# First batch, weight conversion and sixteen feed-forward steps laid out as one list of ranked tasks

## The chip, the cores and the metric

The kernel runs on one core of a Trainium2 chip. A core has a matrix engine (TensorE, "PE" in the profile, its weight loads "PEld"), a vector engine (VectorE, "DVE"), a scalar engine (ScalarE, "ACT"), a general engine (GpSimd, "POOL") and a queue that issues transfers (SyncE, "SP"). Each runs its own instructions in order and waits for the others through semaphores. The metric is the device time of one execution in microseconds (us); a change is judged by the median over several executions.

## The reference

```python
def _attn_ref(q, k, v):                      # q, k, v: 8 batches, 8 heads, 576 tokens, 64
    q_d = q.reshape(B, H, Sd, factor, D).mean(axis=3)      # factor 4: 144 coarse tokens
    ...                                      # k_d, v_d in the same way
    out_d = sm_attn(q_d, k_d, v_d)           # softmax attention over the coarse tokens
    out_up = np.repeat(out_d, factor, axis=2)
    mask = np.abs(pos[:, None] - pos[None, :]) < factor    # each token sees 7 neighbours
    scores = scale * np.matmul(q, k.transpose(0, 1, 3, 2))
    scores = np.where(mask, scores, -1000000000.0)
    ...                                      # softmax
    return out_up + np.matmul(attn, v)

def _moe_ref(x, w_in, w_out, alpha):         # x: 4608 tokens, 512; 2048 hidden
    h = x @ w_in
    g = np.maximum(h, 0.0) + alpha * np.minimum(h, 0.0)
    return g @ w_out
```

The attention of all heads, laid side by side, is the x of the feed-forward. The two weight matrices arrive as 64-bit floats, everything else as 32-bit floats.

## The kernel before

**Feed-forward.** The 4608 tokens are cut into 18 chunks of 256 and the hidden layer into 8 pieces of 256. A step s is one piece of one chunk (s = 8 x chunk + piece): `hidden` (24 matmuls, L752), then `slopes` on ACT, `larger` on DVE (L764), `split` into a high part on ACT and a low part on POOL, then `product` (12 matmuls of 512 columns, L796). Below h(s) and o(s) stand for the hidden and the product of step s. Each operand is held as a high and a low part, so each of the two products is three matmuls. There are 144 steps. A chunk's o sums eight steps in two banks of PSUM.

**Weights.** A 64-bit weight is rebuilt as a 32-bit one by integer operations in `make` (L161): an absolute value on ACT (L184), a clamp and a shift on DVE (L188, L189), sign and low bits on DVE (L193, L194), the high part on ACT (L199, L203) and the low part on DVE (L207, L211). Each of the 16 pieces (8 of w_in, 8 of w_out) holds 1024 elements a partition. Pieces 0 to 4 of each matrix are made whole with their intermediate in SBUF; pieces 5 to 7 in halves, with the intermediate in PSUM banks q and l (L180). Loads (L145, L149) go through three slots.

**First batch.** Batch 0 fills chunks 0 and 1 and 64 tokens ("rest") of chunk 2. It runs over four pairs of heads (`first_batch`, L363). For a pair the queries and keys are turned on PE (L425) and copied by ACT; the neighbour attention runs on PE in nine windows of 64 tokens (L445, L493, L509); the coarse sums of q and k are made on DVE (L453, L455) and turned again on PE (L460); the coarse result is weighed on PE (L501), copied, and added to the neighbour result on DVE (L512).

**Later batches.** The coarse attention is `down` (L224), four times a batch: six loads, two additions each on POOL (L241, L242), a turn on PE (L250), scores, exponentials, weighing (L297). The neighbour attention is `local` (L566), by units of 192 tokens, three units a batch, nearly all on DVE: products with keys (L591), sums (L595), products with values (L643, L647), running sums (L650, L653). Its result is turned on PE (L659), joined with the coarse result on DVE (L671) and placed as a chunk's operand by ACT (L685) and POOL (L69). Units count from 3, the first of batch 1; chunk 2 is the rest of batch 0 and unit 3. `FAR` says how many of a unit's seven neighbours are summed on POOL.

**Order.** Two ways of setting the order stand side by side. The first batch, the first ten pieces and the first `down` are emitted one after another and ordered by the scheduler of the language. From there on each function is given a time counted in steps by `at`, the list is sorted by it, and each engine runs its part in that order: h(s) at s - 1.95, o(s) at s + 0.6, the units at the times of `UNITS`, the last six pieces from `T0_DEC` on. The steps go in order of s, chunk 0 first, then chunk 1.

## Time and profile before

| | us |
|---|---|
| median of 3 runs | 1029.55 |
| lowest, highest | 1028.1, 1031.91 |
| the profiled execution | 1026.39 |
| its span in the trace | 1024.5 |

The span lies inside the execution: 1.89 us stand outside it. In the profile's rows the first number is the start or the busy time, and "[x <-Y]" is the idle time of the engine before the row and what ended it. In the tables by stretch, each engine's busy time stands with its number of instructions, then the granted clock of PE as a share of full speed, then the share of the DMA engines and GB/s.

### The profile page before, as it was taken

Reading aid. Unit: us, or ns where it says so; the run is one execution under the profiler, and the core shown is the slowest. Engines: PE = TensorE matmul, PEld = TensorE weight load, DVE = VectorE, ACT = ScalarE, POOL = GpSimd, SP = SyncE. Lnnn points to the kernel's source line nnn. Section 1 sums busy time; section 2 is a strip of 40 time slices with the busy share of each in tenths; the row PEclk is TensorE's granted clock in tenths of the full one; section 3 lists DMA queues with packets and bytes.
Section 4 is the critical chain, followed back from the end, with each engine's and each line's share of the span. In section 5 each row is a group of like instructions: output and inputs, shape, how many; then the busy total and the mean of one; then the engine's idle time right before and its main releaser. Section 6 shows DMA issues by size and latency. Waiting matters only on the chain.

```text
span 1024.5 us, 17852 instructions
## 1 busy us (share of the span) xinstructions
PE 960.5 (94%) x6402; PEld 853.0 (83%) x6402; DVE 831.8 (81%) x1346; ACT 560.4 (55%) x1484; POOL 487.7 (48%) x612
## 2 busy tenths in 40 slices
...
GB/s 184 228 141 246 111 126 110 96 109 85 115 100 95 106 75 86 109 93 102 107 84 74 92 107 77 116 90 80 104 98 81 93 78 62 73 36 21 1 21 20
DMA packets 59549, 98.25 MB, mean 96 GB/s; under 512 B 19910, under 2 KB 25286, under 8 KB 59462
## 3 DMA queue, kind: packets, MB, share of 16 engines
...
## 4 chain that ended last, share of the span: by engine, by line
PE 74%; DVE 12%; DMA 4%; ACT 3%; issue 2%; SPq 2%; POOL 2%; ACTq 0%; DVEq 0%; POOLq 0%
PE h L752 34%; PE o L796 33%; PE s L263 2%; PE pv L297 2%; DVE temp L193 2%; DMA raw<-in_moe_w_in 1%; PE xp L659 1%; DMA ld<-in_v 1%; PE pT L287 1%; DVE temp L194 1%; DMA k<-in_k 1%; DVE t L764 1%; DVE qk L591 1%; SPq L393 1%; DVE temp L188 1%
## 5 line engine op out<-in xcount | busy, mean ns | idle before, releaser
L69 POOL TENSOR_TENSOR gl<-t,gh 128x512 fp32r<-128x512 f32 x144 | 186.4, 1295 | 312.9 <-ACT gh L769 281.5
L760 ACT ACTIVATE t<-h,slope 128x256 f32<-128x256 f32 x288 | 136.3, 473 | 205.4 <-PE h L752 163.6
L72 POOL TENSOR_TENSOR ld<-ld 72x256 f32<-72x256 f32 x168 | 130.8, 779 | 158.4 <-DMA ld<-in_q 88.6
L752 PE MATMUL h<-xh,wih 128*128 128x256 f32 x1152 | 191.9, 288 | 0.7 <-ACT xh L518 0.7
L764 DVE TENSOR_TENSOR t<-h,t 128x512 f32<-128x512 f32 x144 | 99.0, 687 | 114.8 <-ACT h L761 112.9
L796 PE MATMUL o<-woh,gh 128*128 128x512 f32 x576 | 187.5, 407 | 0.4 <-ACT woh L203 0.4
L752 PE MATMUL h<-xl,wih 128*128 128x256 f32 x1152 | 184.3, 282 | 1.4 <-POOL xl L69 1.4
L752 PE MATMUL h<-xh,wil 128*128 128x256 f32 x1152 | 185.0, 283 | 0.0
L796 PE MATMUL o<-woh,gl 128*128 128x512 f32 x576 | 181.1, 396 | 0.9 <-POOL gl L69 0.9
L796 PE MATMUL o<-wol,gh 128*128 128x512 f32 x576 | 181.4, 396 | 0.2 <-DVE wol L211 0.2
L752 PEld LDWEIGHTS h<-xh,wih 128*128 128x128 f32 x1152 | 164.2, 191 | 10.7 <-issue 1.8
L752 PEld LDWEIGHTS h<-xl,wih 128*128 128x128 f32 x1152 | 157.5, 190 | 1.6 <-POOL xl L69 1.6
L752 PEld LDWEIGHTS h<-xh,wil 128*128 128x128 f32 x1152 | 158.4, 191 | 0.0
L769 ACT CAST gh<-t 128x512 fp32r<-128x512 f32 x144 | 89.1, 619 | 120.7 <-DVE t L764 71.4
L595 DVE TENSOR_REDUCE ls<-qk 128x12 f32<-128x768 f32 (+1 forms) x126 | 136.4, 1082 | 2.8
L796 PEld LDWEIGHTS o<-woh,gl 128*128 128x128 f32 x576 | 108.2, 188 | 27.5 <-POOL gl L69 1.3
L796 PEld LDWEIGHTS o<-wol,gh 128*128 128x128 f32 x576 | 108.1, 188 | 26.8 <-DVE wol L211 1.1
L761 ACT ACTIVATE h<-h,sign 128x256 f32<-128x256 f32 x288 | 126.4, 439 | 0.0
L650 DVE TENSOR_TENSOR lb<-lb,pv 128x384 f32<-128x384 f32 x202 | 113.9, 564 | 5.5
L796 PEld LDWEIGHTS o<-woh,gh 128*128 128x128 f32 x576 | 98.1, 189 | 16.2 <-issue 2.2
L647 DVE TENSOR_TENSOR pv<-v,lb 128x1152 f32<-128x1152 f32 x84 | 93.6, 1115 | 2.6
L591 DVE TENSOR_TENSOR qk<-k,qp 128x768 f32<-128x768 f32 (+1 forms) x78 | 84.1, 1079 | 0.6 <-DMA k<-in_k 0.6
(146 smaller groups left out, 1108.6 us busy)
## 6 DMA issues: line engine op xcount, KB each, us to landing
...
```

The costliest lines, as they stand in the source:

```text
L69: nc.gpsimd.tensor_tensor(o, a, b, op=ALU.subtract)
L72: nc.gpsimd.tensor_tensor(o, a, b, op=ALU.add)
L591: nc.vector.tensor_tensor(st["pr"][:, :nd], window(tiles[u, "k"], half, d0, nd), st["qp", half].unsqueeze(1).to_broadcast([128, nd, 2, 192 ...
L595: nc.vector.tensor_reduce(out=st["s"][:, half, d0:d0 + nd, :].rearrange("p a b -> p (a b)"), in_=st["pr"][:, :nd].rearrange("p a h (t d) - ...
L647: nc.vector.tensor_tensor(st["pr"][:, :nd], window4(tiles[u, "v"], half, d0, nd), prob(half, d0, nd), op=ALU.mult)
L650: nc.vector.tensor_tensor(st["acc"], st["acc"], st["pr"][:, i], op=ALU.add)
L752: nc.tensor.matmul(ph[:, j], w[:, m, 128 * o:128 * o + 128], x[:, m, :], start=(i == 0), stop=(i == 11))
L760: nc.scalar.activation(t[:, j], hs[st][:, j], AF.Copy, scale=slope[:, f:f + 1])
L761: nc.scalar.activation(hs[st][:, j], hs[st][:, j], AF.Copy, scale=sign[:, f:f + 1])
L764: nc.vector.tensor_tensor(gs[st], hs.pop(st), gs[st], op=ALU.max)
L769: nc.scalar.copy(gh, t)
L796: nc.tensor.matmul(po, g[:, j, 128 * m:128 * m + 128], wo[w][n][:, o, :], start=(f == 0 and i == 0), stop=(f == NF - 1 and i == 2))
```

## The change

- Everything up to step 15 becomes one list of tasks, each with an engine, a duration, the tasks it depends on and a rank. `planned` lays them out: again and again it takes the task that can begin first, by rank where several can begin at once. The resulting begin times, divided by `STEP`, are merged with the timed events of the rest of the kernel, and each engine runs the merged order. The scheduler of the language no longer orders any of it. Pair tasks have ranks 0 to 3, the ACT tasks of the conversion 4, the steps 5 to 6.75, the coarse attention of batch 1 5.2 to 6.1, and the DVE tasks of the conversion 8 and up.
- The steps of chunks 0 and 1 are interleaved: chunk 1 follows two pieces behind chunk 0 (`LAG`). Chunk 0 sums in the banks q and l, chunk 1 in the banks o.
- Pieces 0 to 5 are made whole, 6 and 7 in halves; no intermediate is in PSUM any more.
- In the first batch the coarse sums of q and k are taken by DVE from the turned tiles in PSUM (`reduce`), the second turn goes, and the coarse result is summed in the same bank as the neighbour result by matmuls that repeat each coarse column four times (`values`), so the addition on DVE goes.
- In `down` of batch 1 the sums of q and k are taken by 32 small matmuls on PE (`gather`) in place of additions on POOL and four turns.
- Unit 3 works in SBUF (`in_sbuf`), since banks q and l hold chunk 0; one of its seven neighbours, not two, is summed on POOL; the load of unit 4's queries is issued later. The masks are built later (`UNITS[3] - 3.0`).
- The later units start 2.2 (unit 3) or 2.6 steps later on the list, and the steps from 16 on 2.6 (`DELAY`).

```diff
-PTB = 1
-FPT = ('ooo', 'ooo', 'ooo', 'oqo')
-FPV = ('ooo', 'ooo', 'ooo', 'qlq')
-EM = 'bbba'
-ORDER = 'i0 a0 a1 b0 o0 a2 b1 a3 b2 i1 b3 o1 i2'
-N_EARLY = 5
-FIRST = (-1.3, 0.3, 3.0, 5.7)
-T0_DEC, D_DEC = 0.5, 0.56
-UNITS = {3: 7.5, 4: 12.2, 5: 17.4, 6: 22.7, 7: 28.0}
+ORDER = 'a0 i0 a1 b0 a2 b1 i1 a3 b2 o0 b3 i2 o1 i3 o2 i4 o3 i5 o4 o5 i6 i7 o6 o7'
+LAG = 2
+DOWN1 = (5.2, 0.3)
+STEP = 6.3
+DELAY = 2.6
+UNITS = {3: 9.7, 4: 14.8, 5: 20.0, 6: 25.3, 7: 30.6}
 U_STEP = 5.92
 BY_HALF = (5, 9, 13, 17, 21)
-FAR = {3: 2, 4: 2, 5: 2, 6: 2}
+FAR = {4: 2, 5: 2, 6: 2}
...
+            if which == 0 or n < 3:
+                t = weights_temp[0][:, slot % 2, 0:512 * len(cs)]
             else:
-                t = bank("ql"[turns[1] % 2], f"temp{which}{fp}{c}").bitcast(I32)
-            turns[1] += 1
+                t = late.tile([128, 512], I32, tag=("x", "xf", "vt")[slot % 3], name=f"temp{which}{fp}{c}")
...
+        def gather(i):
+            if i == 0:
+                if hp == 0:
+                    new_od(b)
+                st["pt"] = bank("d", f"qkT{nm}")
+            for g in range(2):
+                for f in range(FACTOR):
+                    for e, r in enumerate(halves):
+                        nc.tensor.matmul(st["pt"][r, (2 * i + g) * 72:(2 * i + g) * 72 + 72], st[2 * i + e][:, g, f, :],
+                                         ident[:72, :72], start=(f == 0), stop=(f == FACTOR - 1))
...
+            got = []
+            for i in range(6):
+                got.append(task("SP", 0.7, lambda i=i: load(i), *logs["ld"].get(6 * hp + i - LDB, []), *logs["got"][-1:], pr=place["d"]))
+                logs["got"].append(got[-1])
+                if i == 1 or i == 3:
+                    x = i // 2
+                    m = plan("PE", 1.3, lambda x=x: gather(x), *got[-2:], *(turn_of("d") if x == 0 else [m]))
+                    logs["ld"][6 * hp + i - 1] = logs["ld"][6 * hp + i] = [m]
+                elif i > 3:
+                    logs["ld"][6 * hp + i] = [plan("POOL", 1.3, lambda i=i: fold(i), got[-1], *free("v", S2B))]
+            vs = logs["ld"][6 * hp + 4] + logs["ld"][6 * hp + 5]
+            y = plan("ACT", 1.1, operands, m, *free("qd", 1))
+            rings["d"].append((m, [y]))
...
+            def reduce(x, b):
+                if ("s", x) not in g:
+                    g["s", x] = st.tile([128, 2, 72], F32, tag=f"fs{x}", name=f"fs{x}{hp}")
+                nc.vector.tensor_reduce(out=g["s", x][:, b], in_=g["ph", x, b][:, 0:288].rearrange("p (t a) -> p a t", t=4),
+                                        axis=AX.X, op=ALU.add)
...
+            def values(a, b):
+                ps = g["pv", a] = ps_o.tile([128, 512], F32, tag="po", name=f"fpv{hp}{a}")
+                n = 16 * (b - a)
+                for x in range(2):
                     for e, r in enumerate(halves):
...
+                        nc.tensor.matmul(ps[r, 0:4 * n].rearrange("p (n r) -> p n r", r=4), g["vd"][:, e, x],
+                                         g["th", x][:, SD * e + 16 * a:SD * e + 16 * b].unsqueeze(2).to_broadcast([72, n, 4]),
+                                         start=(x == 0), stop=False)
+                for w in range(a, b):
                     for e, r in enumerate(halves):
...
-                    xs.rearrange("p (a r) -> p a r", r=4),
-                    ps[:, 0:WIN * nw].rearrange("p (a r) -> p a r", r=4),
-                    odf[:, 16 * w0:16 * (w0 + nw)].unsqueeze(2).to_broadcast([128, 16 * nw, 4]), op=ALU.add)
...
+                        nc.tensor.matmul(ps[r, WIN * (w - a):WIN * (w - a) + WIN], vw[hp][:, w, e, :],
+                                         g["pT"][:, w, 64 * e:64 * e + 64], start=False, stop=(w == b - 1))
...
+            def upper(a):
+                if a == 8:
+                    nc.scalar.copy(rest[:, hp, :], g["pv", a][:, 0:WIN])
+                else:
+                    nc.scalar.copy(operand(a // 4)[0][:, hp, :], g["pv", a][:, 0:4 * WIN])
+
+            def lower(a):
+                hi, lo = (t[:, hp, :] for t in operand(a // 4))
+                nc.vector.tensor_tensor(lo, g["pv", a][:, 0:4 * WIN], f32(hi), op=ALU.subtract)
...
+        def in_sbuf():
+            lb = one.tile([128, 256], F32, tag="s2q", name=f"lb{u}")
+            st["pw"] = lb[:, 0:84].rearrange("p (a b c) -> p a b c", a=2, b=7)
+            st["mx"], st["sm"], st["rs"] = (lb[:, 84 + 12 * i:96 + 12 * i].rearrange("p (a c) -> p a c", a=2)
+                                            for i in range(3))
+            acc = late.tile([128, 2, 3, 64], F32, tag="pp", name=f"acc{u}", bufs=2)
+            st["acc"] = acc
+            for half in range(2):
+                st["qp", half] = tiles[u, "q"][:, :, 3 * half:3 * half + 3, :].rearrange("p h t d -> p h (t d)")
...
+            at(when["total", str((1, 5, 2))] + 0.04 if u == 3 else half_done + 0.03 if by_half else t0 + 1.0, load_q, u + 1)
...
+            outs[c] = [bank("ql"[m], f"o{c}_{m}") if c == 0 else ps_o.tile([128, DM], F32, tag="po", name=f"o{c}_{m}")
+                       for m in range(T // 128)]
...
+    def planned():
+        begin, end, free = [0.0] * len(tasks), {}, {}
+        left = list(range(len(tasks)))
+        while left:
+            best = {}
+            for i in left:
+                engine, us, f, deps, pr = tasks[i]
+                if all(d in end for d in deps):
+                    r = max([end[d] + (2.0 if tasks[d][0] == "SP" else 0.15 if tasks[d][0] != engine else 0.0)
+                             for d in deps] + [0.0])
+                    t = max(r, free.get(engine, 0.0))
+                    best[engine] = min(best.get(engine, (1e9,)), (t, pr, i))
+            t, _, i = min(best.values())
+            engine, us = tasks[i][:2]
+            begin[i], end[i] = t, t + us
+            free[engine] = t + us
+            left.remove(i)
+        return begin
...
+        if whole:
+            wait = slots[-3] if len(slots) >= 3 else []
+        else:
+            wait = list(last) + halves_of.get((fp, c), [])
+        got = task("SP", 4.0 * size, lambda slot=len(slots): load_raw(which, fp, cs, slot), *wait, pr=n)
...
+        m = task("ACT", 1.1 * size, lambda: step(0), got, *wait, pr=4 + 0.01 * n)
+        b = m
+        for i, us in enumerate((0.66, 0.66, 1.21, 1.21)):
+            b = task("DVE", us * size, lambda i=i: step(1 + i), b, pr=pr)
+        wait = [signed] if which else []
+        for h in {1: (0, 1), 2: (2, 3)}.get(fp // 2, ()):
+            wait += used[("qk", "vw")[which], h]
+        if fp // 2 == 3:
+            wait += others
+        u = task("ACT", (1.05, 1.45)[which] * size, lambda: step(5), b, *wait, pr=4 + 0.01 * n)
+        d = task("DVE", (1.2, 1.5)[which] * size, lambda: step(6), u, pr=pr)
...
+    order = [x for i in range(NP + LAG) for x in ((0, i), (1, i - LAG)) if 0 <= x[1] < NP]
+    lasts = []
+    for c, fp in order:
+        s = NP * c + fp
+        rank = 5 + 0.1 * len(steps)
+        h = task("PE", 2.9, lambda s=s: hidden(s), *made[0, fp], *turn_of("h"), *(operands[c, hp] for hp in range(4)), pr=rank)
...
+        y = task("PE", 2.9, lambda s=s: product(s), y, *made[1, fp], *free, *steps[-1:], pr=rank + 0.25)
...
+        if s >= 2 * NP:
+            at(DELAY + s - 1.95, hidden, s)
+            at(DELAY + s - 1.45, slopes, s)
+            at(DELAY + s - 1.15, larger, s)
+            at(DELAY + s - 1.0, split, s, 0)
+            at(DELAY + s - 0.99, split, s, 1)
+            at(DELAY + s + 0.6, product, s)
...
+    begin = planned()
+    zero = begin[steps[-1]] - STEP * (2 * NP - 0.4)
+    program = [((b - zero) / STEP, i, t[2], ()) for i, (b, t) in enumerate(zip(begin, tasks))]
+    program += [(t, len(tasks) + i, f, args) for i, (t, f, args) in enumerate(events)]
+    program.sort(key=lambda e: e[:2])
+    end = max(program.index(e) for e in program if e[1] in last) + 1
...
```

551 lines of the change are left out of this document (322 added, 229 removed).

## Prediction

> **What bounds the kernel now.** I began with the page's busy times, then cut the span into stretches, then followed PE's and DVE's rows in order of time. The page, row by engine (busy us, share, instructions):
>
> ```profile
> PE 960.5 (94%) x6402; PEld 853.0 (83%) x6402; DVE 831.8 (81%) x1346; ACT 560.4 (55%) x1484; POOL 487.7 (48%) x612
> ```
>
> PE carries the kernel, but it isn't equally full everywhere. The table by stretch, cut where step 0, unit 3 and step 16 start:
>
> ```profile
> core 0: us, PE busy (x) PEld busy (x) DVE busy (x) ACT busy (x) POOL busy (x), PEclk, DMA share, GB/s
> 9.76:85.96 76.20, 57.53 (x423) 47.83 (x423) 69.04 (x122) 50.96 (x129) 18.87 (x12) 0.76 0.76 193
> 85.96:157.49 71.53, 63.48 (x387) 55.18 (x387) 60.80 (x93) 47.86 (x119) 30.53 (x42) 0.90 0.47 149
> 157.49:200.81 43.32, 40.54 (x275) 35.63 (x275) 38.33 (x58) 25.05 (x68) 27.21 (x35) 1.00 0.31 104
> 260.00:1024.50 764.50, 741.18 (x4929) 662.30 (x4927) 604.50 (x967) 399.20 (x1065) 363.26 (x443) 0.99 0.24 80
> ```
>
> From 260 us on PE is busy 741.18 of 764.50 us at full clock and DVE 604.50: PE bounds this part, and the change doesn't touch it (the units and steps from 16 on keep their order). All it can win lies before. There DVE (69.04 of 76.20, 60.80 of 71.53) is the fuller engine, and PE is idle and partly at a lower clock. The rows at the cuts, from the timelines of PE and DVE (start, length, what):
>
> ```profile
> 9.79 1.19 PE L425 MATMUL f0T<-ident,fqk 72*128 72x72 f32 x8 [9.79 <-DMA fqk<-in_q]
> 85.96 0.58 PE L752 MATMUL h<-xh,wih 128*128 128x256 f32 x1 [0.69 <-ACT xh L518]
> 157.49 1.32 DVE L591 TENSOR_TENSOR qk<-k,qp 128x1152 f32<-128x1152 f32 x1
> 200.81 0.64 PE L752 MATMUL h<-xh,wih 128*128 128x256 f32 x4
> 203.69 0.63 PE L796 MATMUL o<-woh,gh 128*128 128x512 f32 x2
> 206.49 0.64 PE L752 MATMUL h<-xh,wih 128*128 128x256 f32 x4
> 212.21 0.63 PE L796 MATMUL o<-woh,gl 128*128 128x512 f32 x2
> 254.04 0.74 PE L752 MATMUL h<-xl,wih 128*128 128x256 f32 x4 [1.43 <-POOL xl L69]
> ```
>
> PE starts at 9.79; the steps begin in earnest at 85.96; unit 3 starts on DVE at 157.49, when the conversion is over; h(16), which needs unit 3, starts at 200.81; o(15) ends soon after 212.21; h(24), which needs units 4 and 5, waits until 254.04.
>
> **The yardstick.** After h(16) the old order still holds o(14) and o(15); in the new one o(15) at 15.6 precedes h(16) at 16.65. o(14) runs from 203.69 to 206.49, 2.8 us; both together take 5.6. So h(16) of the new kernel is compared with 200.81 + 5.6 = 206.4: each us that it comes earlier is a us won, each us later one lost. Two routes set its time, DVE through unit 3 and PE through its own queue; the later one counts.
>
> **DVE's route.** Groups of DVE instructions up to 210 us (count | busy us, mean ns):
>
> ```profile
> L453 DVE TENSOR_TENSOR fqk<-fqk 72x512 f32<-72x512 f32 x8 | 5.9, 744 | 0.4 <-PE f0T L425 0.4
> L455 DVE TENSOR_TENSOR fs2k<-fqk 72x256 f32<-72x256 f32 x4 | 2.2, 546 | 0.0
> L455 DVE TENSOR_TENSOR fs2q<-fqk 72x256 f32<-72x256 f32 x4 | 1.7, 418 | 0.1
> L512 DVE TENSOR_TENSOR fxs<-fpv,fod 128x256 f32<-128x256 f32 x8 | 3.3, 412 | 0.0
> L512 DVE TENSOR_TENSOR rest<-fpv,fod 128x64 f32<-128x64 f32 x4 | 0.8, 212 | 0.0
> L485 DVE TENSOR_REDUCE fsm<-fp 128x9 f32<-128x630 f32 x4 | 3.2, 798 | 0.0
> L188 DVE TENSOR_SCALAR temp<-temp 128x1024 f32<-128x1024 f32 x10 | 6.8, 683 | 3.2 <-ACT temp L184 3.2
> L188 DVE TENSOR_SCALAR temp<-temp 128x512 f32<-128x512 f32 x12 | 8.3, 692 | 2.6 <-ACT temp L184 2.6
> L189 DVE TENSOR_SCALAR temp<-temp 128x1024 int32<-128x1024 int32 x10 | 7.8, 782 | 0.1
> L189 DVE TENSOR_SCALAR temp<-temp 128x512 int32<-128x512 int32 x12 | 8.4, 699 | 0.4
> L764 DVE TENSOR_TENSOR t<-h,t 128x512 f32<-128x512 f32 x17 | 11.6, 682 | 0.3 <-ACT h L761 0.2
> L647 DVE TENSOR_TENSOR pv<-v,lb 128x384 f32<-128x384 f32 x2 | 1.1, 554 | 0.1
> L650 DVE TENSOR_TENSOR lb<-lb,pv 128x384 f32<-128x384 f32 x8 | 4.5, 563 | 0.2
> L100 DVE TENSOR_SCALAR mask_l<-pat_l,fl_l 128x84 f32<-128x84 f32 x1 | 0.8, 764 | 0.0
> ```
>
> - Coarse sums of q and k: L453 and L455 go, 5.9 + 2.2 + 1.7 = 9.8 us. In their place come 16 reductions of 288 elements. The nearest row is L485, 798 ns for 630: by elements 365 ns, together 5.8 (at most 12.8, a whole L485 each; at least 2.9, half of that share). Net -4.0.
> - The addition of the coarse result (L512) goes: -3.3 - 0.8 = -4.1. The low part is then taken from PSUM, with as many elements as before; I cost that at nothing.
> - Conversion: a half in PSUM costs L188 692 and L189 699 ns, a whole piece in SBUF 683 and 782. Piece 5 of both matrices made whole saves 4 x 1.39 - 2 x 1.465 = 2.6; eight halves moved to SBUF save 1.39 - 0.73 = 0.66 each if a half costs half a whole, 5.3 (nothing if it doesn't). Together -7.9, between -2.6 and -7.9. The other three steps go by elements: unchanged.
> - Added before unit 3: the masks (0.8 for L100 on the left, about 0.5 for the rest), the split of pair 3's softmax in two (three more short operations, 0.6), and some two L764 more (1.4), since chunk 1 runs earlier. +3.3.
> - Unit 3 itself gets 1.9 longer: one neighbour comes back from POOL, two more products (L647, 0.4 more each in a joint instruction) and two sums (L650, 0.56 each).
>
> Net before unit 3: -4.0 - 4.1 - 7.9 + 3.3 = -12.7 of 69.04 + 60.80 = 129.8 us, so 117.1. Between 9.76 and 157.49 lie 147.7 us; 17.9 are idle. Who ended them (waits of DVE up to 210 us: total, times, longest):
>
> ```profile
> DVE wol L211 <- ACT woh L203: 6.8, 4, 3.0
> DVE temp L188 <- ACT temp L184: 5.8, 6, 2.0
> DVE fv L471 <- DMA fv<-in_v: 5.4, 3, 2.6
> ```
>
> These are ACT running its conversion tasks too late, and a load. Rank 4 puts these ACT tasks ahead of the steps, and DVE gets other work in the gaps; the DMA share falls from 0.76 to 0.47 after the first stretch, so transfers have room, though the first 60 us stay tight. I keep half, 9 us. Unit 3 then starts at 9.8 + 117.1 + 9 = 136, and h(16), 43.3 + 1.9 later, could start at **181**. Ends: 172 with no idle time, 202 with all of it, no gain on halves and dear reductions (5.3 + 7.0 more).
>
> **PE's route.** The change gives PE work. Groups of PE instructions up to 210 us:
>
> ```profile
> L297 PE MATMUL pv<-th,s2v 72*64 72x144 f32 x32 | 3.4, 339 | 0.0
> L250 PE MATMUL qkT<-ident,s2q 72*128 72x72 f32 x10 | 1.7, 254 | 3.7 <-ACT th L291 2.7 <-POOL gl L69 1.0
> L501 PE MATMUL fdv<-th,fvd 72*64 72x144 f32 x32 | 4.1, 383 | 1.7 <-ACT th L340 1.7
> L460 PE MATMUL fsum<-ident,fs2k 72*128 72x72 f32 x8 | 1.8, 328 | 0.0
> L460 PE MATMUL fsum<-ident,fs2q 72*128 72x72 f32 x8 | 1.7, 299 | 3.1 <-ACT kT L433 2.6 <-DVE fs2q L455 0.4
> ```
>
> L297 stands for 4 products of 144 columns in each of four `down`: 576 columns in 0.85 us. `gather` has 32 products of 72 columns, 2304 columns: 3.4 us in place of the turns' 0.68 (L250 for q 1.7 / 5, for k as much). Four times +2.7: +10.9. `values` takes the coarse part over 2304 columns a pair where L501 had 576: by L297 3.4 x 4 = 13.6, less L501's 4.1: +9.5 (by L501's own rate +12.3). L460 goes: -3.5. o(14) and o(15) now come first: +5.6. From 9.76 to 200.81 PE was busy 57.53 + 63.48 + 40.54 = 161.6 of 191.1 us; with these 184.1. But part of it ran slowly: 57.53 x 0.24 + 63.48 x 0.10 = 20.1 us were lost to the clock (an estimate from the table's mean clocks), and 29.5 us were idle, together 49.6. The work at full clock is 184.1 - 20.1 = 164, so h(16) comes at 9.8 + 164 = 174 plus whatever idle and slow time is left. The old first stretch holds 18.7 idle and 13.8 slow, 32.5 of the 49.6: PE waited there for a first batch that shared DVE with the conversion. Ranks 0 to 3 put the pairs first, and later each piece of a weight serves two steps, so that PE has twice the work per piece. But the pairs are still chains over four engines. I keep half of the first stretch, 16, and 2 of the rest: h(16) at 174 + 18 = **192**. Ends: 4 left over gives 178, all 49.6 gives 223.
>
> What a wait costs in clock shows in PE's timeline (start, length, idle before):
>
> ```profile
> 95.37 0.98 PE L263 MATMUL s<-kd,qd 128*96 128x144 f32 x6 [1.86 <-ACT kd L258]
> 96.84 1.05 PE L752 MATMUL h<-xh,wil 128*128 128x256 f32 x4
> 194.19 0.44 PE L659 MATMUL xp<-ident,x 128*128 128x128 f32 x2 [1.73 <-ACT kd L258]
> 194.94 0.63 PE L752 MATMUL h<-xh,wil 128*128 128x256 f32 x4
> ```
>
> After a wait of 1.86 us four matmuls take 1.05 us, after one of 1.73 still 0.63. So a gap near 2 us can cost the gap and then some 1.7 us more, until the clock is back. The Trainium skill, "TensorE: Matmul & The Clock Gate", What's actually happening, ties the half clock to an idle window of about 3.4 us and the way back to as long a busy one; by it only long gaps would cost clock, 8 of my 18 us would go, and the sum would be 8 us lower. The 1.86 us row speaks against so mild a reading, and I stay with the row.
>
> **Hidden parts.** ACT loses the two scaled copies of unit 3 and a copy a pair and gains next to nothing; with 124 us busy of 191 it has room. POOL, busy 76.6 of 191, loses the additions of q and k: nothing. New waits: o(0) now waits for banks q and l, which pair 3's shift frees, and o(8) for the banks o, which pair 3's results free; h, products and turns queue behind them on PE, but both banks are free before the operands of chunk 0 are complete. The load of unit 4's queries, moved behind unit 3's last sum, has some two steps of the list to land; without that cover the start of unit 4 slips by what is missing. The six loads of each `down` stand in SP's one queue between the weights: a late one holds the weight behind it. h(24) follows: DVE reaches it 254.04 - 157.49 + 1.9 = 98.5 after unit 3's start, at 234.5; PE, from 192 and with 5.6 us less before it, at about 239 to 240. PE is the later here too.
>
> **The sum.** PE's route ends last: 192 against 206.4, a gain of 14.4. Span 1024.5 - 14.4 = 1010.1, with the 1.89 us outside it an execution of 1012; against the median of the runs, which is 3.2 above the profiled one, 1029.55 - 14.4 = **1015**.
>
> **The rivals.**
> - A, forecast, 0.52: 1015, own range 1006 to 1023 (idle and slow time 9 to 26).
> - B, PE stays warm and packed, 0.20: both routes meet near 178, gain 28, 1001. For it: the decoding of one piece now feeds 11 us of PE work in place of 5.6. Against it: first pairs that wait for their loads, as at 9.79.
> - C, the plan doesn't do what it says, 0.16: the engines run their list in order, actual lengths differ from the planned ones, and each late task holds those behind it, so DVE keeps all its 17.9 idle us and PE some 30 of its 49.6: h(16) near 204, 1027. For it: the idle rows of DVE are all waits for an engine that was busy elsewhere.
> - D, PE becomes the bound of the first part, 0.12, slower: the 20.4 us that `gather` and `values` add lie on PE before h(16), and gaps of 2 us or more in the plan bring back the half clock behind each. From 32.4 us of idle and slow time on the change loses; at 45 h(16) comes at 219, 1042. For it: 49.6 before; against it: the added work itself fills gaps.
>
> The range takes in A, most of B and C: 1000 to 1033. About 0.5% (5 us) is what a measurement here can tell from no change. Faster by more (below 1024.4): A and B, 0.72. Within it: C, 0.16. Slower: D, 0.12.
>
> **What would show it.** Right: h(16) between 183 and 200; unit 3 on DVE between 126 and 146; no L453, L455 and L512 of old; PE's clock in the first 86 us above 0.85; the part after h(24) as long as before. Wrong: `gather` or `values` at half speed and far over 3.4 us each; DVE idle above 17.9 us before unit 3; PE idle after h(16), where the list leaves 3.6 steps between o(15) and o(16); a first weight piece that lands late because a `down` load holds SP.

## The result, and the profile after

The changed kernel is slower: 1064.01 us, median of four executions (1058.47 to 1065.79), beside 1029.88 for the kernel before (four executions). The ratio is 1.0322, with a 95% interval of 1.0276 to 1.0367. The forecast was 1015, its range ended at 1033. Two of all executions reported here, both of e1 (1111.9 and 1118.2 us), ran in a slower state and are left out of every comparison.

The profiled execution took 1062.31 us with a span of 1060.5, 36.0 us more than the 1024.5 of before. The page's row by engine, and PE's, DVE's and the clock's shares by stretch, cut where PE starts, where step 0 starts, where unit 3 starts on DVE and where step 16 starts (columns as in the prediction):

```profile
PE 991.1 (93%) x6690; PEld 877.1 (83%) x6690; DVE 840.2 (79%) x1335; ACT 560.2 (53%) x1476; POOL 467.2 (44%) x576
```

```profile
5.77:90.34 84.57, 72.48 (x500) 60.04 (x500) 55.86 (x103) 46.57 (x120) 1.10 (x1) 1.00 0.60 149
90.34:178.57 88.23, 76.86 (x595) 69.06 (x594) 78.98 (x102) 58.22 (x131) 31.02 (x34) 0.90 0.45 145
178.57:231.19 52.62, 42.85 (x305) 36.08 (x304) 42.99 (x60) 22.44 (x63) 23.67 (x28) 0.92 0.30 99
```

PE starts 4 us earlier than before, and everything behind that is later: h(0) at 90.34, unit 3 at 178.57 in place of 157.49, h(16) at 231.19 in place of 206.4 on the prediction's yardstick. That yardstick shows 24.8 of the 36 us; the rest arises behind h(16). In the first stretch PE is busy for 72.48 of 84.57 us and DVE for only 55.86; before, DVE was the full one there (69.04 of 76.20).

**Where the 36 us arise.** The units run on DVE one after another, so their starts are a better ruler than h(16). The first two of them after, from DVE's timeline:

```profile
178.57 1.89 DVE L736 TENSOR_TENSOR qk<-k,q 128x1152 f32<-128x1152 f32 x1
217.88 1.34 DVE L736 TENSOR_TENSOR qk<-k,qp 128x1152 f32<-128x1152 f32 x1
```

Read off in the same way in all kernels of this study (us):

| | h(0) | unit 3 | 4 | 7 | 9 | from 9 to the end |
|---|---|---|---|---|---|---|
| before | 86.0 | 157.5 | 188.5 | 295.2 | 369.6 | 654.9 |
| after | 90.3 | 178.6 | 217.9 | 333.4 | 406.0 | 654.5 |

From unit 9 on the two kernels are the same to 0.4 us. The loss is 21.1 us ahead of unit 3, 8.3 between units 3 and 4, 8.8 between 4 and 7, and 1.8 come back between 7 and 9.

**Two things that the page doesn't say aloud.** The first is PE's clock. The column shows 1.00 for 5.77 to 90.34, but the rows don't: the scores of five windows (ten rows, since the profile lists each of these products twice) take 2.25 us at 14 us and at 53 us, where e1 below has 1.23 at full speed; four products of h take 1.06 us at 91.4 and 0.64 from 93.7 on.

```profile
13.97 2.25 PE L491 MATMUL fs<-kT,qb 128*128 128x70 f32 x10
52.95 2.25 PE L491 MATMUL fs<-kT,qb 128*128 128x70 f32 x10
```

```profile
L491 PE MATMUL fs<-kT,qb 128*128 128x70 f32 x72 | 16.2, 410 | 0.0
L610 PE MATMUL fpv<-th,fvd 72*64 72x256 f32 x64 | 15.5, 639 | 0.0
L615 PE MATMUL fpv<-fpT,vw 70*64 70x64 f32 x144 | 10.2, 314 | 0.0
L610 PE MATMUL fpv<-th,fvd 72*64 72x64 f32 x32 | 2.6, 318 | 0.0
```

The second fence is PE's groups up to 100 us. `values` (L610 and L615) takes 15.5 + 10.2 + 2.6 = 28.3 us. So the whole first batch ran at half speed, and a clock that had not changed since the start left no mark in the column. The same holds for the kernel before. The scores of its first pair, from PE's timeline, and two stretches of its first 86 us:

```profile
13.54 4.11 PE L445 MATMUL fs<-kT,qb 128*128 128x70 f32 x18
```

```profile
9.79:35.00 25.21, 20.50 (x105) 18.57 (x106) 20.42 (x36) 14.16 (x38) 0.00 (x0) 1.00 0.96 188
52.00:85.96 33.96, 22.01 (x155) 16.69 (x153) 33.65 (x57) 22.25 (x54) 15.29 (x11) 0.50 0.49 168
```

4.11 us for 18 rows is 0.228 each, as much as 2.25 for ten. So the old kernel, too, ran at half speed up to 35 us, where its column shows 1.00, and again from 52 to 86. The half speed did not come with the change; the change put more of PE's work into it.

The second thing that the page doesn't say is DVE's conversion, of which three groups up to 215 us are shown here, those of before first:

```profile
L193 DVE SCALAR_TENSOR_TENSOR temp<-raw,temp 128x1024 int32<-128x1024 int32 x10 | 12.7, 1266 | 0.1
L211 DVE SCALAR_TENSOR_TENSOR wol<-temp,sign,woh 128x512 fp32r<-128x512 f32 x16 | 11.8, 757 | 6.8 <-ACT woh L203 6.8
```

```profile
L190 DVE SCALAR_TENSOR_TENSOR temp<-raw,temp 128x1024 int32<-128x1024 int32 x12 | 18.0, 1499 | 0.2
L211 DVE SCALAR_TENSOR_TENSOR wol<-temp,sign,woh 128x512 fp32r<-128x512 f32 x16 | 16.1, 1039 | 0.5 <-ACT woh L203 0.4
L182 DVE TENSOR_SCALAR temp<-temp 128x512 f32<-128x512 f32 x8 | 3.9, 488 | 5.1 <-ACT temp L178 5.1
```

The same operations are up to 37% longer on average; all groups of the conversion together take 97.8 us where they took 94.5. The averages hide two kinds. Of the twelve L190 on a whole piece in after, the six with no two-operand instruction of POOL beside them take 1.22 us each, the other six 1.78; of the sixteen L211, nine take 0.74 and seven, beside POOL, 1.42.

**Behind unit 3** POOL stands still, and PE behind it. POOL's, SP's and PE's timelines of after:

```profile
196.99 0.83 POOL L772 TENSOR_TENSOR pv<-v,lex 128x384 f32<-128x384 f32 x1 [6.68 <-DVE lex L764]
211.02 0.72 POOL L69 TENSOR_TENSOR ld<-ld 72x256 f32<-72x256 f32 x1 [13.21 <-DMA ld<-in_v]
...
214.22 1.26 POOL L66 TENSOR_TENSOR gl<-t,gh 128x512 fp32r<-128x512 f32 x1
```

```profile
194.94 1.16 SPq L667 DMA_DIRECT2D q<-in_q  x2
196.14 1.63 SPq L686 DMA_DIRECT2D k<-in_k  x2
197.87 1.13 SPq L233 DMA_DIRECT2D ld<-in_v  x1
```

```profile
215.53 1.22 PE L951 MATMUL o<-woh,gl 128*128 128x512 f32 x2 [7.25 <-POOL gl L66]
```

POOL waits 13.21 us for a v load of the fourth `down`. SP issued it right behind unit 4's queries and keys, two loads of 192 KB and two of 384 KB, 1.15 MB in all; the DMA queues moved near 100 GB/s from 196 to 210, which is 11.5 us for these bytes. Behind the waiting fold stand unit 3's last product on POOL and a gl, and o waits 7.25 us for that gl.

### The profile page after: what moved, and what is told of

The parts are those of the page before. It is cut to its first block, busy times and chain, and to the rows that moved or that the text cites. A ratio compares the mean times of both kernels' runs of the same rounds, so it can differ in the third digit from the quotient of the medians.

```text
span 1060.5 us, 18341 instructions
## 1 busy us (share of the span) xinstructions
PE 991.1 (93%) x6690; PEld 877.1 (83%) x6690; DVE 840.2 (79%) x1335; ACT 560.2 (53%) x1476; POOL 467.2 (44%) x576
## 4 chain that ended last, share of the span: by engine, by line
PE 71%; DVE 11%; DMA 7%; POOL 4%; ACT 3%; issue 3%; SPq 0%; ACTq 0%; POOLq 0%; DVEq 0%
PE o L951 30%; PE h L900 30%; DMA ld<-in_v 4%; DMA ld<-in_k 2%; PE fpv L610 2%; PE fs L491 1%; DVE temp L190 1%; PE s L264 1%; PE pv L298 1%; POOL ld L69 1%; PE pT L288 1%; DVE qk L736 1%; DVE ls L740 1%; PE xp L804 1%; POOL gl L66 1%
## 5 line engine op out<-in xcount | busy, mean ns | idle before, releaser
L66 POOL TENSOR_TENSOR gl<-t,gh 128x512 fp32r<-128x512 f32 x144 | 191.3, 1329 | 307.1 <-ACT gh L923 274.9
L69 POOL TENSOR_TENSOR ld<-ld 72x256 f32<-72x256 f32 x152 | 115.5, 760 | 205.9 <-DMA ld<-in_v 147.0
L951 PE MATMUL o<-woh,gl 128*128 128x512 f32 x576 | 183.5, 400 | 13.5 <-POOL gl L66 13.5
L795 DVE TENSOR_TENSOR lb<-lb,pv 128x384 f32<-128x384 f32 x194 | 109.4, 564 | 5.2
L736 DVE TENSOR_TENSOR qk<-k,qp 128x768 f32<-128x768 f32 (+1 forms) x75 | 80.9, 1078 | 2.3 <-DMA k<-in_k 2.3
```

The costliest lines, as they stand in the source:

```text
L66: nc.gpsimd.tensor_tensor(o, a, b, op=ALU.subtract)
L69: nc.gpsimd.tensor_tensor(o, a, b, op=ALU.add)
L736: nc.vector.tensor_tensor(st["pr"][:, :nd], window(tiles[u, "k"], half, d0, nd), st["qp", half].unsqueeze(1).to_broadcast([128, nd, 2, 192 ...
L795: nc.vector.tensor_tensor(st["acc"], st["acc"], st["pr"][:, i], op=ALU.add)
L951: nc.tensor.matmul(po, g[:, j, 128 * m:128 * m + 128], wo[w][n][:, o, :], start=(f == 0 and i == 0), stop=(f == NF - 1 and i == 2))
```

## The experiments

Four theories at the start; a fifth, on unit 3's tiles, came out of the runs. **Clock**: the first batch is bound by a PE at half speed. **Port**: POOL's gl slows DVE's conversion, which now reads SBUF alone. **Queue**: a late operand at the head of POOL's queue holds gl and the units. **Plan**: the lengths given to the planner are wrong, so that the list's order is wrong. Times were taken in six sessions, each beside the kernel before, so ratios are compared. The starts in the table are those of one profiled execution each, the times are medians; that execution was 5.5 us shorter than its median in e4 and 5.0 longer in e13. PE's list of the first batch is the same in after and in e2, e3, e5, e7, e9, e12 and e16, and its h(0) came at 86.2 to 91.1: differences of 5 us at this point are not told apart.

| | edit | h(0) | unit 3 | 4 | 7 | us | ratio [95%] |
|---|---|---|---|---|---|---|---|
| after | | 90.3 | 178.6 | 217.9 | 333.4 | 1064.0 | 1.0322 [1.0276, 1.0367] |
| e1 | products to keep PE busy | 107.9 | 196.7 | 236.2 | 351.4 | 1068.4, 1082.6 | not given |
| e2 | no gl for 16 steps | 91.0 | 173.9 | 210.5 | 326.4 | 1056.9 | 1.0281 [1.0216, 1.0347] |
| e3 | unit 4's loads later | 90.5 | 179.0 | 231.3 | 344.5 | 1073.9 | 1.0442 [1.0400, 1.0485] |
| e4 | measured lengths | 88.1 | 166.6 | 202.4 | 318.6 | 1055.9 | 1.0259 [1.0212, 1.0306] |
| e5 | batch 2's folds later | 86.2 | 175.6 | 213.2 | 335.9 | 1067.1 | 1.0355 [1.0298, 1.0411] |
| e6 | coarse result apart | 75.7 | 170.0 | 213.2 | 327.9 | 1058.4 | 1.0273 [1.0233, 1.0314] |
| e7 | chunk 1 behind chunk 0 | 90.7 | 178.7 | 217.1 | 331.1 | 1062.8 | 1.0311 [1.0259, 1.0362] |
| e8 | e4 + e5 | 88.6 | 170.0 | 206.5 | 328.1 | 1060.5 | 1.0296 [1.0255, 1.0337] |
| e9 | s2q free, folds as before | 90.0 | 178.3 | 222.7 | 332.9 | 1063.7 | 1.0361 [1.0333, 1.0389] |
| e10 | e4 + e6 | 81.4 | 166.0 | 215.6 | 328.6 | 1056.1 | 1.0277 [1.0243, 1.0311] |
| e11 | e10 + e9 | 77.6 | 161.3 | 221.0 | 329.8 | 1064.4 | 1.0362 [1.0329, 1.0396] |
| e12 | order of loads, s2q free | 87.1 | 176.8 | 214.9 | 325.7 | 1057.4 | 1.0269 [1.0235, 1.0304] |
| e13 | e12 + e6 | 75.0 | 169.2 | 210.8 | 322.8 | 1052.2 | 1.0215 [1.0182, 1.0247] |
| e14 | e12 + e4 + e6 | 78.6 | 163.7 | 207.1 | 315.7 | 1049.1 | 1.0186 [1.0158, 1.0215] |
| e15 | e12 + e4 | 88.7 | 168.6 | 206.5 | 313.9 | 1047.0 | 1.0169 [1.0137, 1.0201] |
| e16 | e7 + unit 3 in PSUM | 91.1 | 179.8 | 215.3 | 327.6 | 1056.5 | 1.0260 [1.0218, 1.0302] |
| e17 | e16 + e4 + loads | 88.7 | 172.2 | 206.2 | 316.5 | 1048.1 | 1.0179 [1.0139, 1.0220] |
| e18 | e17 + e6, unit 3 listed later | 79.8 | 168.0 | 199.5 | 308.5 | 1039.3 | 1.0088 [1.0059, 1.0117] |

### The first batch and PE's clock: e1, e6

e1 puts products whose results are overwritten ahead of the real ones:

```diff
+        def warm(ps, n):
+            for _ in range(n):
+                nc.tensor.matmul(ps, unit, unit, start=True, stop=True)
+
+        warm(ps_h.tile([128, 512], F32, tag="ph", name="warm")[:, 0:128], 40)
...
+                warm(ps[:, 0:128], 6)
                 nc.tensor.matmul(ps, unit, wmask[:, a:b].rearrange("p w j -> p (w j)"), start=True, stop=False)
```

> Adds about 330 short products of unit by unit (128 columns) on PE, ahead of the first flips and before the flips, scores, turns and values of the first batch, in banks that the real products then overwrite. Theory Clock (PE runs the whole first batch at half speed, 5.8 to 93 us, and its list is planned with full-speed lengths: h(0) at 90.3 where the plan has 74.7): with PE kept at full speed the pair of `window_scores` takes under 3.2 us in place of 4.1 to 4.5, h(0) comes at 75 to 82, and the time falls to 1046 to 1054. Rival Chain (the first batch is a chain over ACT, DVE and loads, PE's speed is covered): h(0) stays at 88 to 95 and the time within 5 us of 1064 or above. If PE stays slow even when never idle, h(0) goes past 100.

Measured: 1068.4 and 1082.6 us, h(0) at 107.9 in the profiled execution (1082.6), the last of the three cases. PE's timeline in e1:

```profile
2.38 8.80 PE L396 MATMUL warm<-unit 128*128 128x128 f32 x40 [2.38 <-ACT unit L390]
...
25.60 2.25 PE L499 MATMUL fs<-kT,qb 128*128 128x70 f32 x10
...
39.02 1.52 PE L396 MATMUL f1T<-unit 128*128 128x128 f32 x6
...
40.88 0.87 PE L396 MATMUL f1T<-unit 128*128 128x128 f32 x6
...
49.66 1.23 PE L499 MATMUL fs<-kT,qb 128*128 128x70 f32 x10
```

There is no wait between 2.38 and 50, yet the clock is half until 40; then the scores of five windows fall from 2.25 to 1.23. So the half speed is shown, and so is what full speed is worth, but being busy was not enough to get there, and the added products, at 0.22 us each in the slow part, cost more than they could bring. The run doesn't decide between Clock and Chain.

e6 takes PE work away instead. The coarse part gets its own bank, a copy and an addition, as it was:

```diff
-                        nc.tensor.matmul(ps[r, 0:4 * n].rearrange("p (n r) -> p n r", r=4), g["vd"][:, e, x],
-                                         g["th", x][:, SD * e + 16 * a:SD * e + 16 * b].unsqueeze(2).to_broadcast([72, n, 4]),
-                                         start=(x == 0), stop=False)
...
+                        nc.tensor.matmul(g["po"][r, 0:SD], g["vd"][:, e, x], g["th", x][:, SD * e:SD * e + SD],
+                                         start=(x == 0), stop=(x == 1))
...
+                g["od"] = st.tile([128, SD], F32, tag="odf", name=f"fod{hp}")
+                nc.scalar.copy(g["od"], g["po"][:, 0:SD])
...
+                nc.vector.tensor_tensor(xs.rearrange("p (a r) -> p a r", r=4),
+                                        g["pv", a][:, 0:WIN * (b - a)].rearrange("p (a r) -> p a r", r=4),
+                                        g["od"][:, 16 * a:16 * b].unsqueeze(2).to_broadcast([128, 16 * (b - a), 4]), op=ALU.add)
```

> Undoes the summing of both attentions in one bank: the coarse result of a pair is made by four products of 144 columns in a bank of its own, copied by ACT, and added by DVE (12 additions more). Theory Clock (the first batch is bound by a PE at half speed, so PE work is worth twice its planned length): values falls from 28.3 us to near 10 + 4, h(0) comes 8 to 13 us earlier than 90.3, DVE is 4 us busier, time 1050 to 1057. Rival Chain (waits between engines set the first batch; four products and twelve additions change little): h(0) within 4 us, time 1060 to 1070.

Measured: 1058.4 us, just above the 1050 to 1057 named, and h(0) at 75.7, 14.6 us earlier, more than the 8 to 13. PE's groups of `values` up to 100 us:

```profile
L626 PE MATMUL fpv<-fpT,vw 70*64 70x64 f32 x144 | 9.0, 296 | 0.5 <-DVE fxs L618 0.5
L609 PE MATMUL fdv<-th,fvd 72*64 72x144 f32 x32 | 4.8, 454 | 0.0
```

28.3 us have become 13.8: 14.5 us less PE work, and h(0) 14.6 us earlier. That the two agree so closely is chance, for h(0) scatters by 5 us; that the gain is far outside this scatter is not. Clock holds, Chain falls. But unit 3 gains only 8.6 us, and unit 4 4.7, since the stretch from 3 to 4 grows to 43.2.

### DVE's conversion beside POOL: e2

```diff
+            if st < 2 * NP:
+                nc.gpsimd.memset(f32(gl), 0.0)
+            else:
                 sub(gl, t, f32(gh))
```

> For the first 16 steps the low part gl is set to zero by POOL instead of being subtracted from t and gh; that part of the product is left out. Theory Port (POOL's two-operand subtraction slows DVE's conversion, whose operands all lie in SBUF: 97.8 us after against 94.5 before and 86.6 expected): the DVE conversion falls to 84 to 90 us, L190 whole from 1.50 to near 1.27, L211 from 1.04 to near 0.76, and unit 3 starts 6 to 12 us earlier than 178.6. Rival Size (these operations are simply this long in SBUF): conversion stays at 96 to 99 us and unit 3 at 176 to 180. The end also gains from o not waiting for gl (10 us of waits of PE before 260 us).

DVE's groups of e2 up to 215 us:

```profile
L190 DVE SCALAR_TENSOR_TENSOR temp<-raw,temp 128x1024 int32<-128x1024 int32 x12 | 14.7, 1222 | 0.2
L211 DVE SCALAR_TENSOR_TENSOR wol<-temp,sign,woh 128x512 fp32r<-128x512 f32 x16 | 12.0, 786 | 0.4 <-ACT woh L203 0.4
```

1499 becomes 1222 and 1039 becomes 786, as expected; the whole conversion falls from 97.8 to 90.5 us, half a microsecond above the range named, and unit 3 starts 4.7 us earlier, short of the 6. Port holds for 7.3 us. The other 3.9 us down to the 86.6 of my forecast are not gl's: an operation on a half piece is no half of one on a whole piece (L182: 0.515 here for a half, 0.83 for a whole). The end isn't compared, since o also no longer waits for gl.

### One chunk behind the other: e7

```diff
-LAG = 2
+LAG = 8
```

> Undoes the interleaving of the two chunks: all eight steps of chunk 0, then all eight of chunk 1, the rest planned by the same rule. If running two chunks per weight is what fills PE (my prediction: each piece serves 11 us of products in place of 5.6), the run is slower than after by 5 to 20 us, 1069 to 1084. If it only moves work, since PE was bound by the first batch and later by unit 3's chain, the time stays at 1059 to 1069; if two open steps are what makes gl, t and h wait for each other, it falls below 1058.

Measured: 1062.8, the middle case. Running two chunks per piece doesn't fill PE: unit 3 and the time are the same without it.

### The planner's lengths: e4

```diff
-        for i, us in enumerate((0.66, 0.66, 1.21, 1.21)):
+        for i, us in enumerate((0.79, 0.72, 1.5, 1.24) if whole else (0.49, 0.58, 0.84, 0.69)):
...
-                m = pe(0.3 + 0.22 * (b - a), lambda a=a, b=b: window_scores(a, b), *ready, *turn_of("ql"[a > 0]))
+                m = pe(0.4 + 0.45 * (b - a), lambda a=a, b=b: window_scores(a, b), *ready, *turn_of("ql"[a > 0]))
...
-                m = pe(0.1 + 0.45 * (b - a), lambda a=a, b=b: values(a, b), flat[a], loaded["w", hp], *ths, v2, *turn_of("o"))
+                m = pe(0.15 + 0.66 * (b - a), lambda a=a, b=b: values(a, b), flat[a], loaded["w", hp], *ths, v2, *turn_of("o"))
```

> Only the durations that the planner is given are changed, to those measured after: scores of windows 0.4 + 0.45 a window (was 0.3 + 0.22), values 0.15 + 0.66 (0.1 + 0.45), conversion 0.79, 0.72, 1.5, 1.24 and 1.25 or 2.08 for a whole piece, gl 1.75; the first `down` starts behind the last pair's turns and the end of chunk 0 goes ahead of later work. By the planner's own rule h(0) is then at 93.8 and o(15) at 204.9 (was 74.7 and 182.9; 90.3 and 223.9 on the chip). Theory Plan (the list is in the wrong order because its lengths are wrong, and each engine holds work behind late tasks): h(16) comes 8 to 20 us earlier, time 1044 to 1056. Rival Work (the order costs little; there is more work on a slow PE and DVE): within 6 us of 1064.

The diff shows the main lines; e4 also lets the first `down` start behind the last pair's turns and moves the end of chunk 0 ahead of later work.

Measured: h(16) at 217.6, 13.6 us earlier, and unit 3 at 166.6, 12.0 earlier, in an execution that was itself 5.5 us below its median. By the ratios the gain is 0.63 of the 3.22%, a fifth of the loss, and the two intervals overlap; the same edit on e12 (e15) takes off 1.00, and there they don't. So part of the loss lies in the order. In e4 the conversion ends on DVE at 156.0, 1.5 us earlier than in the old kernel; unit 3 follows only 10.6 us later, since DVE first waits 8.05 us for the scores of a `down`. The lengths that were wrong are PE's in the first batch: the old ones are those of full speed (e1 has a pair of window scores at 0.99 and 1.25 us from start to start, the list 1.18 and 1.40; after has 2.0 and 2.5).

### POOL's queue: e3, e5, e8, e9, e11

Five runs that each took one thing out of POOL's way, and none of them gained. (e8 is compared with e4, e11 with e10.) e3 moves unit 4's loads; e5 the second batch's `down`, whose first fold needs the slot s2q that unit 3 holds:

```diff
-            at(when["total", str((1, 5, 2))] + 0.04 if u == 3 else half_done + 0.03 if by_half else t0 + 1.0, load_q, u + 1)
-            at(when["total", str((1, 5, 2))] + 0.05, load_kv, u + 1, "k")
+            at(when["total", str((1, 5, 2))] + 0.94 if u == 3 else half_done + 0.03 if by_half else t0 + 1.0, load_q, u + 1)
+            at(when["total", str((1, 5, 2))] + (0.95 if u == 3 else 0.05), load_kv, u + 1, "k")
```

```diff
-            down(b, hp, first + (end - first - 0.5) * hp / 4 - (2.0 if b == 2 else 4.5), 0.45)
+            down(b, hp, first + (end - first - 0.5) * hp / 4 - ((-0.3, 0.8, 1.6, 2.0)[hp] if b == 2 else 4.5), 0.45)
```

> The loads of unit 4's queries and keys are issued 0.9 steps later in the list, behind the v load of the fourth `down` pair. Theory Queue (that v load stood behind them on SP, POOL waited 13.2 us for it with gl behind, and PE waited 7.25 us for gl): POOL's 13.2 us wait at 198 to 211 is under 5, h(16) comes 4 to 9 us earlier than 231.2, time 1054 to 1060. Rival Shift (unit 4 starts later by what its loads are later, or the wait only moves): h(16) within 3 us or h(24) as late as before, time 1061 to 1067.

> The second batch's `down` pairs start 1.7, 1.2, 0.4 and 0 steps later in the list, so that POOL's fold of its first q (whose slot s2q is held by unit 3's new SBUF tile lb until unit 3's last product on DVE) no longer stands ahead of the last gl. In after that slot is taken at 213.0, in the run with later loads POOL waited 9.0 us there, with measured lengths 11.4 us. Theory Fold (POOL's queue is held by this slot, and h(16) with it): POOL has no wait for a DVE product before h(16), h(16) 4 to 9 us earlier than 231.2, time 1055 to 1060. Rival Load (in after the v load of the fourth `down` holds the same place, so that the fold alone gives nothing): POOL's 13.2 us wait stays, h(16) within 3 us, 1061 to 1067.

> Measured lengths for the planner as in the fourth run (1055.9), and the later start of the second batch's `down`. There POOL waited 11.4 us at 188 to 199.5 for unit 3's product with the last gl and unit 3's far product behind it. Theory Fold: that wait goes, h(16) falls from 217.6 to 208 to 214 and the time to 1046 to 1053. Rival: the last gl waits for something else as long, 1053 to 1058.

POOL's timelines of e3 and of e5 in the same place:

```profile
211.24 0.76 POOL L69 TENSOR_TENSOR s2q<-ld 72x128 f32<-72x128 f32 x1 [8.99 <-DVE pv L792]
```

```profile
207.01 1.05 POOL L69 TENSOR_TENSOR ld<-ld 72x256 f32<-72x256 f32 x1 [11.80 <-issue]
```

With the loads moved, the v load is there by 201, and the fold behind it waits 8.99 us for unit 3's slot; the keys of unit 4 then arrive so late that it starts at 231.3. With the folds moved, POOL stands 11.80 us; the row names no cause, but the v load was again issued right behind unit 4's queries and keys, at 192.9. Two holds in one place: each alone shows only the other. The times of e3 (1073.9) and e8 (1060.5) lie above both ranges named, that of e9 (1063.7) in the rival's and that of e5 (1067.1) at the rival's upper end. In e5 and e8 h(16) did come 9.1 and 15.3 us earlier than in after, and the end did not: in e5 the steps then stood on PE behind batch 2's turns and weighing (waits of 3.50 us at 250 and 2.11 at 258), DVE waited for these steps (5 to 6 took 43.7 us in place of 36.2), and at 329 it waited 7.59 us for POOL's product of unit 6. So h(16) is no measure of the end, which is why the table goes by units.

e9 gives unit 3's sums tiles of their own and puts the folds back to 2.7 steps; e11 adds this to e10.

```diff
-            lb = one.tile([128, 256], F32, tag="s2q", name=f"lb{u}")
-            st["pw"] = lb[:, 0:84].rearrange("p (a b c) -> p a b c", a=2, b=7)
...
+            st["mx"], st["sm"], st["rs"] = (one.tile([128, 12], F32, tag=f"l{x}", name=f"l{x}{u}").rearrange("p (a c) -> p a c", a=2)
+                                            for x in ("mx", "sm", "rs"))
...
+                if u == 3:
+                    st["pw"] = st["ex"]
```

> Unit 3's small sums get tiles of their own (its weights are written over its exponentials), so that the slot s2q is free for the second batch's folds, and these stand where they stood in before (2.7 steps ahead of the unit, after had 2.0). Nothing else is changed. Unit starts on DVE: from 3 to 4 31.0 us before, 39.3 after; from 6 to 7 37.0 before, 43.4 after, where DVE waited 7.4 us for POOL's product of unit 6, which stood behind a fold that waited for a v load. Theory Fold: both holds of POOL shrink, 3 to 4 takes 34 to 37 us and 6 to 7 37 to 40, time 1053 to 1059. Rival Load: the folds wait for their loads wherever they stand, both stretches stay within 2 us, 1060 to 1068.

> The separate coarse result of e6 (h(0) 75.7, unit 3 170.0, 1058.4) with the measured lengths of e4 (h(0) 88.1, unit 3 166.6, 1055.9). If the half-speed PE work of the first batch and the wrong lengths are two causes that add, unit 3 starts at 155 to 161 and the time is 1044 to 1051; if both are the same thing (a plan that is short of the first batch's PE lengths), unit 3 starts at 163 to 168 and the time is 1052 to 1058.

> e10 with e9's free slot and place of the folds. If POOL's queue is a cause of its own behind unit 3, the time is 5 to 11 us below e10's; from 6 to 7 the units take 37 to 40 us. If it isn't, within 3 us of e10.

The earlier folds put still more loads ahead of the v load: in e9 POOL waits 18.2 us for it and 3 to 4 takes 44.4. From 6 to 7 it takes 34.8 us in place of 43.4 and from 5 to 6 41.5 in place of 36.2, 3.3 gained together. In e10 unit 3 starts at 166.0, no earlier than in e4, and the time is no lower (1056.1): it is the second case, in which both edits mend the same thing. Unit 4 starts at 215.6, whatever unit 3 does. There unit 3 starts before the conversion is over, and 5.4 us of it run inside the stretch from 3 to 4, as in e14 (in e11 5.5, in e6 and e13 1.5, elsewhere 0.1 at most). e11 has unit 3 at 161.3 and unit 4 at 221.0, and at 1064.4 it lies 8 us above e10, outside both cases.

### The order of loads mended: e12 to e15

e12 takes both holds away: e3's edit, e9's tiles, and the second batch's first loads behind the v load ((0.7, 1.4, 2.2, 2.7) in place of e5's four numbers).

> The order of loads around unit 3 alone: the last v loads of the first `down` four stand ahead of unit 4's queries and keys (0.9 steps later) and of the second batch's first loads (1.3 steps later), and unit 3's sums have tiles of their own so that no fold waits for s2q. Theory Queue (POOL waits 13.2 us for a v load that stands behind 1.15 MB at near 100 GB/s, with gl and unit 3's far product behind it): no wait of POOL over 5 us between unit 3 and unit 4, unit 4 starts at 211 to 214 in place of 217.9 (33 to 36 us after unit 3), time 1054 to 1060. Rival Ring (the loads wait for their three slots, not for the queue): POOL's wait stays over 10 us, time 1061 to 1068.

> e12 with the separate coarse result (e6: unit 3 at 170.0, then 43.2 us to unit 4, 1058.4). Theory Queue: unit 4 at 203 to 207, time 1045 to 1052. Rival Ring: unit 4 stays at 211 to 216, time over 1055.

> e13 with the measured lengths (e10: unit 3 at 166.0, then 49.6 us to unit 4, 1056.1). Theory Queue: 33 to 37 us from unit 3 to unit 4, unit 4 at 199 to 203, time 1041 to 1049, still above the 1027 of the kernel before. Rival Ring: unit 4 at 210 to 216 and over 1054.

> e12 with the measured lengths (e4: unit 3 at 166.6, 35.8 us to unit 4, 1055.9, where POOL's hold was already short of e12's). Theory Queue expects little here: unit 4 at 200 to 203, time 1052 to 1057; a gain above 4 us would say that the hold costs more than the 11 us seen in POOL's waits.

POOL's timeline of e12 in the place of the 13.21 us:

```profile
203.57 1.20 POOL L772 TENSOR_TENSOR pv<-v,lex 128x384 f32<-128x384 f32 x1 [4.65 <-DVE x L798]
204.74 2.40 POOL L66 TENSOR_TENSOR gl<-t,gh 128x512 fp32r<-128x512 f32 x1
```

The wait for the v load is gone, PE waits 0.44 us for gl in place of 7.25, and all four runs are 0.5 to 0.9% below the same kernel with the old loads; for e14 and e15 the intervals don't overlap. Queue is right about the wait, and Ring falls. But the time was not won where Queue had put it. From unit 3 to unit 4 it takes 38.1, 41.6, 43.4 and 37.9 us in e12 to e15, not the 33 to 37 named. The gain lies behind: from 4 to 7 it takes 110.8, 112.0, 108.6 and 107.4 us, where the same kernels with the old loads took 115.5, 114.7, 113.0 and 116.2 and the old kernel 106.7. e9, which shares the free slot but not the order of loads, has 110.2 there, so this gain is not shown to be the order's. e15 gained more than I had expected (1052 to 1057). Between units 3 and 4 I had missed something: DVE is now busy for 36.7 of the 38.1 us, in after for 33.1 of 39.3, in the old kernel for 28.7 of 31.0.

### Unit 3's tiles: e16 to e18

DVE's groups between units 3 and 4, of e12 and then of e16:

```profile
L795 DVE TENSOR_TENSOR acc<-acc,pv 128x384 f32<-128x384 f32 x10 | 8.9, 885 | 0.3
L734 DVE TENSOR_TENSOR qk<-k,q 128x1152 f32<-128x1152 f32 x2 | 3.4, 1675 | 0.0
```

```profile
L795 DVE TENSOR_TENSOR lb<-lb,pv 128x384 f32<-128x384 f32 x8 | 4.5, 565 | 0.2
L736 DVE TENSOR_TENSOR qk<-k,qp 128x1152 f32<-128x1152 f32 x2 | 2.7, 1344 | 0.0
```

Both operands of unit 3's sums lie in SBUF since the change, for its banks went to the interleaved chunk 0. In after this cost the sums nothing, since POOL stood waiting for the v load. The same group in after, and then the ten sums of e12 one by one, from DVE's timeline:

```profile
L795 DVE TENSOR_TENSOR acc<-acc,pv 128x384 f32<-128x384 f32 x10 | 5.6, 556 | 0.3
```

```profile
199.05 1.73 DVE L795 TENSOR_TENSOR acc<-acc,pv 128x384 f32<-128x384 f32 x3
201.68 1.15 DVE L795 TENSOR_TENSOR acc<-acc,pv 128x384 f32<-128x384 f32 x2
206.03 3.28 DVE L795 TENSOR_TENSOR acc<-acc,pv 128x384 f32<-128x384 f32 x3
210.74 2.91 DVE L795 TENSOR_TENSOR acc<-acc,pv 128x384 f32<-128x384 f32 x2
```

While POOL stands still (198.9 to 203.57 in e12) each of five sums takes 0.54 to 0.56 us; once it works again, the other five take 0.70 to 1.91, 1.22 on average. So the price of the tiles came to light only when POOL's wait was gone, and took back what that had won here. e16 gives unit 3 its banks again, which also frees the slot s2q, and hands one neighbour back to POOL:

```diff
-LAG = 2
+LAG = 8
-FAR = {4: 2, 5: 2, 6: 2}
+FAR = {3: 2, 4: 2, 5: 2, 6: 2}
...
-        if u == 3:
+        if u < 0:
             at(t0 - 0.6, in_sbuf)
```

> On the changed kernel: chunk 1 behind chunk 0 (so that the banks q and l come free at the end of chunk 0), unit 3's queries, weights and sums in these banks again, and two neighbours of unit 3 on POOL as before; chunk 0's copy out goes ahead of later work. e7, without unit 3's tiles, gave 1062.8 and 38.4 us from unit 3 to 4. Theory SBUF (tiles in SBUF cost unit 3 some 5 to 9 us of DVE beside POOL): DVE busy from unit 3 to unit 4 falls from 34 to 30 us, the stretch to 31 to 35, time 1054 to 1060. Rival: POOL's wait for the v load sets this stretch whatever DVE does: 37 to 41 us and 1060 to 1066.

> e16 with the measured lengths and the order of loads of e12 (e15 without e16's edits: 1047.0, 37.9 us from unit 3 to unit 4, DVE busy for 36). Theory SBUF: 31 to 34 us, unit 4 at 199 to 202, time 1038 to 1044. Rival: 36 or more, 1045 to 1050.

> e17 with the separate coarse result, and unit 3 placed 0.9 steps later in the list since the banks come free later there (e14 without e16's edits: 1049.1, unit 3 at 163.7, 43.4 us to unit 4). Everything of the change that cost time in my reading is then undone but the conversion in SBUF and `gather`. Theory SBUF: 31 to 35 us from unit 3 to unit 4, time 1034 to 1042; it would still not reach the 1027 to 1030 of before, since POOL's gl slows the conversion. Rival: unit 3 starts later by what its place in the list gives up, 1044 to 1050.

A sum takes 565 ns and a product 1344; DVE is busy for 28.1 us between units 3 and 4. Part of that is the neighbour on POOL, for which the prediction had 1.9 us. In e16 the stretch is 35.5 us; 5.4 of it are one wait of DVE for the scores of a `down`. e17 gains nothing on e15 and lies in the rival's range: the stretch falls to 34.0, but unit 3 starts 3.6 us later. In e18 the stretch is 31.5, what it was before (31.0), and the time 1039.3, the best of all and 0.9% above before. No version here beats the old kernel.

In shares of the old kernel's time, after stands at +3.22%. Alone, e4 takes off 0.63, e6 0.49, e12 0.53 and e16 0.62; the interval of each overlaps that of after, so none of them is shown by its time alone. e18, which has all four but e12's tiles, takes off 2.34, far outside the intervals. So it is shown that the four together hold most of the loss, but not how it divides among them. The sum of the four, 2.27, comes near by luck, for the runs between do not add: e6 on top of e4 gives nothing (e10 is 0.18 above e4, e14 0.17 above e15), e16's edits on top of e15 give nothing either (e17 is 0.10 above it), and e6 with e16's edits takes off 0.81 (e18 below e15).

Of e18's +0.88% the place is known: its unit 3 starts at 168.0 in place of 157.5, 10.5 of the 14.2 us by which its span is longer. DVE is busy there for 136.2 us from 6.0 on where the prediction's table has 129.8 from 9.8 on, the conversion is still at 96.6 us, and DVE waits 5.73 us for unit 3's queries. Whether halves in PSUM would win that back, and what `gather` costs in the end, was not tried.

## Why the prediction was wrong

**"I keep half of the first stretch, 16, and 2 of the rest: h(16) at 174 + 18 = 192."** This step failed. PE ran 225.4 us from its start to h(16); less my 164 at full clock, 61.4 us were idle or slow where I had kept 18, more even than the 49.6 that I had counted in the old kernel. And by the rows both counts are too low. Idle were 33.2 us (225.4 less the busy 72.48 + 76.86 + 42.85 = 192.2). With the first stretch at half speed, some 47 us were slow (72.48 / 2 + 76.86 x 0.10 + 42.85 x 0.08, an estimate as in the prediction), which makes 80, and 145 of work at full clock. In the old kernel 29.3 were slow, not 20.1 (half of the 20.50 up to 35 us, of the 3.40 from 41.8 to 45.2 and of the 22.01 from 52 on, and 6.3 in the second stretch); with the 29.5 idle that is 58.8, and 132 of work. So the change did not halve the idle and slow time of PE; it added more than 20 us to it. My 164 of work was 19 too high, which hid part of this. I took the gain from the ranks and from two steps per piece; e7 shows that the second is worth nothing, and e6 that the first stretch was set by the length of PE's own work at half speed.

**The work added to PE** was priced at full speed and done at half. `gather` took 12.0 us in after, against 13.6. `values` took 28.3, against 22.2 to 25.0 (the old 12.7, of which 4.1 are L501 and 8.6 its neighbour part, and my 9.5 to 12.3 more); at full speed it would be 13.9, by e1's rows from 42.39 to 47.04 without the added products. I set this work against gaps; on a PE that was the bound it counted in full (14.5 us less work, 14.6 earlier in e6).

**The clock.** I read the mean of 0.76 in the first stretch of before as time lost in short gaps that a fuller PE would close. The mean was itself too high, for it counts 25 us of half speed as full. e1 closed the gaps and the clock stayed at half for 38 us. The sign that I had named for success, a clock above 0.85 in the first 86 us, stood in the column with 1.00 while the rows ran at half; of my signs of failure two came, `values` at 7.1 us a pair and DVE's idle time. The Trainium skill, "TensorE: Matmul & The Clock Gate", What's actually happening, which the prediction weighed, has the full clock after some 3.4 us of sustained work. h(0) alone would agree with it (it starts at 90.3 and is fast from 93.3 on), but PE had been at work without a wait since 82.5, and e1's 38 us do not agree. Why the products of the first batch don't bring the full clock is open.

**DVE's conversion, -7.9:** it came out at +3.3, the largest error among the terms of DVE's work. "0.66 each if a half costs half a whole" failed (0.488 for 0.789), and I let the halves move from PSUM to SBUF for nothing. The Trainium skill, "SBUF — State Buffer", Who interferes with whom, says that a DVE instruction with two inputs in SBUF contends with a GpSimd instruction that reads SBUF; e2 agrees, 7.3 us, and so do the sums of e12 (1.22 us on average beside POOL, 0.56 without it); L207 does not show it, at 1.22 us with POOL and without. I hadn't looked for this rule, though it speaks against two parts of the change.

**"I keep half, 9 us"** of DVE's 17.9 idle: by the table of after it was 28.7 (84.57 less 55.86) in the first stretch, where PE was the bound, and 9.3 in the second, 38.0 in all. Two other terms held: the sums of q and k took 7.0 us against 5.8 expected, and the additions of L512 are gone.

**"h(16), 43.3 + 1.9 later", and the part behind it unchanged.** It took 52.6 us, and units 4 to 7 lost 8.8 more. Between units 3 and 4, DVE was busy 4.4 us longer than before (33.1 against 28.7), of which I had 1.9 for the neighbour, and idle 3.9 longer; POOL's wait of 13.2 us, with gl and unit 3's last product behind it, wasn't in the sum, nor was a price for tiles in SBUF. I named "a `down` load holding SP" as a sign of failure, for the first weight pieces; it was a fold holding POOL. From unit 9 on nothing changed, as said.

**The rivals.** C had the mechanism, late tasks holding those behind them, but I let it end at the old kernel's idle time, at 1027. D had the sign and half of the reason: PE did become the bound, and the point of decision, 32.4 us of idle and slow time, was passed by 29 in the prediction's own sum. But the half clock was not brought back by gaps in the plan; it lasted from the start. My upper end, 45, was below what the old kernel itself had shown, 49.6; a plan with new lengths could do worse than the order it replaced, and I had left that out.
